# Linear attention and two feed-forward layers on one core: weighted sums made token by token, low parts on GpSimd, one written order for all engines

## The chip, the core and the metric

The kernel runs on one core of a Trainium2 chip. A core has five engines that run side by side, each through its own queue in order: PE (TensorE, matrix products and transposes), DVE (VectorE), ACT (ScalarE), POOL (GpSimd) and SP, which here only starts transfers. Products land in PSUM (eight banks of 128 partitions x 512 f32 numbers), everything else lives in SBUF. The metric is the time of one execution in microseconds (us) on the device.

## The reference

Attention without a softmax over tokens: queries and keys are turned into positive features, the keys' features are summed against v once per head, and every token's output is a weighted sum divided by its own denominator. Two feed-forward layers follow.

```python
batch, n_heads, seq, head_dim = (4, 8, 576, 64);  d_feat = 128
def phi(x):
    proj = np.einsum('bhsd,df->bhsf', x, w_phi)
    proj = proj - np.max(np.abs(proj), axis=-1, keepdims=True)
    return np.concatenate([np.exp(proj), np.exp(-proj)], axis=-1)
q_p, k_p = (phi(q), phi(k))
kv = np.einsum('bhsf,bhsd->bhfd', k_p, v)
z = np.sum(k_p, axis=2)
num = np.einsum('bhsf,bhfd->bhsd', q_p, kv)
den = np.einsum('bhsf,bhf->bhs', q_p, z)[..., None] + 1e-06
x = (num / den)                     # then batch and tokens become 2304 rows of 512
gate = 1.0 / (1.0 + np.exp(-(x @ w_gate)));  x = gate * (x @ w_val) @ w_out      # d_ff 1536
h = x @ w_in2;  out = np.maximum(0.01 * h, h) @ w_out2                           # d_ff 2048
```

## The kernel before

**Attention.** The work goes by pairs of heads, `B * KD` = 16 of them (four batches, four pairs each). Of a batch's 576 tokens 512 are the main part and 64 the remainder; the remainders of two pairs are handled together. For a pair: `t_main` transposes k and q (8 transposes, `ps_t`), ScalarE copies them to `x`; `p_k` and `p_q` project (`ps_p`), VectorE takes the largest magnitude (`m`, L337) and subtracts it (`t`, `tq`, L339), ScalarE takes Exp with both signs (`ka` for keys); `q_f` transposes the queries' differences (`ps_q`) and ScalarE writes the features `qf` from there; `kv_main` sums keys' features against v and a column of ones (`kv`, 36 short products, copied to `kvz`). Then `num` streams all 576 tokens through the summed matrix (`ps_n`, features already the right way round, 288 tokens a product, copied to `u`), `den` streams them through the column of sums (`ps_d`, copied to `dd` on VectorE). The denominators go round through memory: `norm1` stores four rows of `dd` into `d` with nine to a partition, `norm2` adds, inverts, stores to `rd` and reads it back spread over 64 partitions (`rb`), and GpSimd multiplies (L443). `norm3` splits the result into a high part in the reduced-precision type that PE multiplies at one pass (`xh`, ScalarE) and a low part (`xl`, VectorE, L51 by `split`).

**Gated units.** Every f32 product of the layers is made of three: high x high, high x low, low x high (`mm3`, L54 to L56). While attention runs, the first two hidden blocks (256 columns, `c` = 0) of layer one are made for batches 0 to 2 as soon as their x is ready (`moe_units`: `up1` into the banks `pg` and `pv`, `down1` into the same two), 216 products of 512 columns in all.

**Weights** arrive as 64-bit floats and are decoded in halves of a tile (`decode`: six operations on VectorE and two on ScalarE a half, of which the last, L115, makes the low part).

**Order.** `ORDERS` lists pieces by slot; it fixes the order of PE alone (`manual_schedule` with PE). A `d` asks for two decode steps, an `M` for one group of three gated products. The other engines' order comes from a scheduler. PSUM: two double banks (`pp`), two single ones (`at`), and `pg`, `pv`. After the stage the rest of layer one (from batch 3 of `c` = 0 on, `up_plain`, banks `ps_u`) and layer two follow; the change leaves their code alone.

Of the kernel before, what the change touches and what calls it, by code (L numbers as in the profile page):

```python
# [19 lines left out]
def linear_attention_moe(ctx, tc, q, k, v, w_phi, w_gate, w_val, w_out, w_in2, w_out2, out):  # L20
# [19 lines left out]
    ps_m = ctx.enter_context(tc.tile_pool(name="ps_m", bufs=1, space=PS))  # L40
# [6 lines left out]
    nc.scalar.activation(out=warm, in_=ebias, func=ACTF.Exp)  # L47
# [49 lines left out]

    def decode(raw, m, hi, lo, expo):
# [16 lines left out]
        nc.vector.tensor_tensor(out=lo, in0=mf, in1=hi.bitcast(F32), op=ALU.subtract)  # L115
        yield
# [11 lines left out]

    def decoded(keys, reserve, hold):
# [3 lines left out]
        raws = deque(fetch(keys[n // 2], n % 2, 3) for n in range(3))  # L133
        for n, key in enumerate(keys):
# [73 lines left out]
    def up1(c, b, h):  # L208
        w = bw[b]
        for f in range(CH):  # L210
            fs = slice(128 * f, 128 * f + 128)
            ps = []
            for i in range(2):
                p = ps_m.tile([128, 512], F32, tag=("pg", "pv")[i], name=("pg", "pv")[i])[:, :w]
                ps.append(p)
                wt = wts[1, c, i]
                for kk in range(KD):
                    yield kk
                    mm3(p, wt["vhi"][:, kk, fs], wt["vlo"][:, kk, fs], xpart(xh, b, kk), xpart(xl, b, kk), kk == 0, kk == KD - 1)
                if i == 0:  # L220
                    th = pools["tp"].tile([128, 512], F32, tag="th", name="th")[:, :w]
                    nc.scalar.activation(out=th, in_=p, func=ACTF.Tanh, scale=0.5)
            nc.vector.scalar_tensor_tensor(out=th, in0=th, scalar=1.0, in1=ps[1], op0=ALU.add, op1=ALU.mult)
            hidden(h, (f, b), th)
            yield KD - 1

# [11 lines left out]
    def down1(c, b, h):  # L238
        for e in range(KD):
            po = ps_m.tile([128, 512], F32, tag=("pg", "pv")[e % 2], name="po")[:, :bw[b]]  # L240
            for f in range(CH):
                if f:
                    yield 0
                mm_down1(po, wts[1, c, 2], b, e, h, f)
            first_sum(b, e, po, pools["tp"].tile([128, 512], F32, tag="st", name="st", bufs=2))
            yield
# [13 lines left out]
    def pair_bank(name):  # L260
        return ps_a.tile([128, 2, 512], F32, tag="pp", name=name, bufs=2)
# [20 lines left out]
    def load_pair(b, c):  # L282
        hs = slice(2 * c, 2 * c + 2)
        for nm, src, eng in (("k", k, nc.sync), ("q", q, nc.scalar if b == c == 0 else nc.sync)):
            t = ld.tile([128, J, 2, D], F32, tag=nm, name=nm)
            eng.dma_start(out=t, in_=src[b, hs, 0:MAIN, :].rearrange("h (p j) d -> p j h d", j=J))
            nat[nm, b, c] = t
            if (nm, b, c) == ("k", 0, 0):
                for h in range(2):
                    nc.gpsimd.dma_start(out=wbd[64 * h:64 * h + 64, h * NF:(h + 1) * NF], in_=w_phi)  # L290
        if c % 2 == 0:
            for nm, src in (("k", k), ("q", q)):
                t = ld.tile([128, 2, D], F32, tag=nm + "r", name=nm + "r", bufs=1)
                for h in range(2):
                    nc.sync.dma_start(
                        out=t[64 * h:64 * h + 64],
                        in_=src[b, 2 * c:2 * c + 4, MAIN:S, :].rearrange("(i h) s d -> h s i d", h=2)[h],
                    )
                nat[nm + "r", b, c // 2] = t
        vf = nat["v", b, c] = vfs[c % 2]  # L300
        nc.sync.dma_start(
            out=vf[:, 0:J].rearrange("p j (h w) -> p j h w", h=2)[:, :, :, 0:64],
            in_=v[b, hs, 0:MAIN, :].rearrange("h (p j) d -> p j h d", j=J),
# [4 lines left out]
    class Pair:  # L308
        pass

    rem = {}

    def t_main(p):
        ps = pair_bank("ps_t")
        for i, nm in enumerate("kq"):
            src = nat.pop((nm, p.b, p.c))
            for j in range(J):
                nc.tensor.transpose(ps[:, i, 128 * j:128 * j + 128], src[:, j].rearrange("p h d -> p (h d)"), ident)  # L318
        p.x = xt.tile([128, 2, MAIN], F32, tag="x", name="x", bufs=1)
        if TCOPY[p.i] == "D":  # L320
            nc.vector.tensor_copy(p.x, ps)
        else:
            nc.scalar.copy(p.x, ps)

    def t_rem(p):
        if p.c % 2:
            return
        ps = one_bank(256, "ps_tr")
        for i, nm in enumerate("kq"):
            nc.tensor.transpose(ps[:, 128 * i:128 * i + 128], nat.pop((nm + "r", p.b, p.c // 2)).rearrange("p i d -> p (i d)"), ident)  # L330
        rem["x"] = xt.tile([128, 256], F32, tag="xr", name="xr", bufs=1)
        nc.scalar.copy(rem["x"], ps)

    def centred(ps, shape, tag, bufs):

        m = wk.tile([128] + shape[:-1], F32, tag="m" + tag, name="m", bufs=2)
        nc.vector.tensor_reduce(out=m, in_=ps, axis=AX.X, op=ALU.max, apply_absolute_value=True)  # L337
        t = wk.tile([128] + shape, F32, tag=tag, name=tag, bufs=bufs)
        nc.vector.tensor_tensor(out=t, in0=ps, in1=m.unsqueeze(len(shape)).to_broadcast([128] + shape), op=ALU.subtract)  # L339
        return t  # L340

    def proj(x, tag):

        ps = pair_bank("ps_p")
        for j in range(J):
            for h in range(2):
# [156 lines left out]
    with tc.manual_schedule(engines={mybir.EngineType.PE}):  # L503
# [19 lines left out]
        for _ in m_gen:  # L523
            pass
# [463 lines left out]
```

## Time and profile before

| | |
|---|---|
| median of 3 runs | 1017.79 us (1016.29 to 1018.81) |
| the profiled execution | 1017.43 us, of which 1015.7 us are the span from first to last instruction |
| busy in the span | PE 982.6 us (97%), DVE 723.4 (71%), ACT 474.9 (47%), POOL 156.0 (15%) |
| granted TensorE clock | 0.995 of full speed on average |

The profiled execution lies 0.36 us under the median. 1.73 us lie outside its span. PE is nearly always busy on paper, but "busy" counts an instruction from its start to a modelled end, so products that follow one another overlap, and a PE that is slowed or handed work late can still look busy. How much work fits into a stretch is better read from the distance between starts.

### The profile page before, as it was taken

How to read it: one execution, taken by the hardware profiler on the slowest of the kernel's cores; microseconds unless marked ns; L12 is line 12 of the kernel's file. 1: busy time of each engine (PE TensorE's matmuls, PEld its weight loads, DVE VectorE, ACT ScalarE, POOL GpSimd, SP SyncE). 2: the span in 40 equal slices, each digit the busy share in tenths (PEclk: the TensorE clock that was granted, in tenths of full speed). 3: DMA queues.
4: the chain of work that ended last, by engine and by line, in shares of the span. 5: the costliest groups of instructions: out<-in, count | busy, mean ns of one | idle time of the engine just before them, and what ended most of it. 6: DMA issues, size and time to landing. Idle time of an engine off the chain costs nothing.

```text
span 1015.7 us, 16203 instructions
## 1 busy us (share of the span) xinstructions
PE 982.6 (97%) x6310; PEld 801.0 (79%) x6310; DVE 723.4 (71%) x1228; ACT 474.9 (47%) x817; POOL 156.0 (15%) x208
## 2 busy tenths in 40 slices
PE   7889899999999999999999999999999999999998
PEld 6556676777788888888888778788888888888886
DVE  4988555454587292974867679998878797978555
ACT  4766455545355344543544434665334343433221
POOL 1011011011002234143231312100101010101000
PEclk8999999999999999999999999999999999999999
DMA  7666444331699579496794956546334251614244
GB/s 191 165 180 160 127 132 111 99 96 46 213 328 282 77 204 179 92 288 100 158 268 71 228 187 248 193 146 201 130 119 165 84 193 56 228 43 165 65 153 136
DMA packets 118173, 160.15 MB, mean 158 GB/s; under 512 B 67504, under 2 KB 70064, under 8 KB 118096
## 3 DMA queue, kind: packets, MB, share of 16 engines
q1 hardware_dynamic: 92800, 93.75, 29.6%
q0 software_dynamic: 24256, 65.09, 25.5%
q8 instruction: 50, 0.82, 0.3%
q10 hardware_dynamic: 1040, 0.26, 0.1%
q14 instruction: 27, 0.22, 0.1%
HBM read 109.64 MB, written 49.36 MB: 157 GB/s over the span
## 4 chain that ended last, share of the span: by engine, by line
PE 75%; DVE 8%; issue 6%; DMA 5%; POOL 3%; ACT 2%; SPq 1%; POOLq 0%; DVEq 0%; ACTq 0%
PE ps_u L55 11%; PE ps_u L56 11%; PE ps_u L54 11%; PE ps_p L54 9%; PE ps_p L55 9%; PE ps_p L56 9%; PE ps_p L348 2%; DMA rb<-rd 2%; PE kv L387 2%; PE ps_n L415 2%; POOL accd L611 2%; DVE m L337 1%; PE ps_t L318 1%; POOL rb L443 1%; DMA w<-td 1%
## 5 line engine op out<-in xcount | busy, mean ns | idle before, releaser
L764 DVE TENSOR_TENSOR q<-ps_u,q 128x512 f32<-128x512 f32 x160 | 109.6, 686 | 63.6 <-PE ps_u L56 57.1
L54 PE MATMUL ps_u<-xh,w 128*128 128x512 f32 (+1 forms) x432 | 150.7, 350 | 1.2 <-ACT xh L50 1.1
L55 PE MATMUL ps_u<-xl,w 128*128 128x512 f32 (+1 forms) x432 | 151.4, 351 | 0.3 <-DVE xl L619 0.3
L56 PE MATMUL ps_u<-xh,w 128*128 128x512 f32 (+1 forms) x432 | 150.9, 350 | 0.0
L834 DVE TENSOR_TENSOR acc<-acc,ps_p 128x512 f32<-128x512 f32 x126 | 86.1, 683 | 39.6 <-PE ps_p L56 39.0
L54 PE MATMUL ps_p<-w,gh 128*128 128x512 f32 x288 | 112.2, 390 | 0.0
L55 PE MATMUL ps_p<-w,gh 128*128 128x512 f32 x288 | 112.0, 389 | 0.0
L56 PE MATMUL ps_p<-w,gl 128*128 128x512 f32 x288 | 111.6, 389 | 0.0
L611 POOL DMA_DIRECT2D accd<-w x80 | 70.7, 889 | 215.8 <-ACT w L610 139.8
L54 PE MATMUL ps_u<-w 128*128 128x512 f32 x256 | 100.4, 392 | 2.4 <-DVE q L764 2.4
L55 PE MATMUL ps_u<-w 128*128 128x512 f32 x256 | 100.0, 390 | 0.7 <-DMA w<-td 0.7
L56 PE MATMUL ps_u<-w 128*128 128x512 f32 x256 | 99.6, 389 | 0.0
L724 POOL DMA_DIRECT2D w<-td x88 | 48.0, 554 | 326.7 <-PE ps_u L56 303.0
L54 PEld LDWEIGHTS ps_u<-xh,w 128*128 128x128 f32 x432 | 81.5, 189 | 13.0 <-ACT xh L50 1.6
L55 PEld LDWEIGHTS ps_u<-xl,w 128*128 128x128 f32 x432 | 81.7, 189 | 12.1 <-DVE xl L619 0.7
L56 PEld LDWEIGHTS ps_u<-xh,w 128*128 128x128 f32 x432 | 81.7, 189 | 10.7
L650 ACT ACTIVATE q<-q 128x512 f32<-128x512 f32 x48 | 30.2, 632 | 113.1 <-DVE q L764 112.8
L54 PE MATMUL ps_p<-gh,w 128*128 128x512 f32 (+1 forms) x216 | 78.4, 366 | 1.9 <-DVE acc L614 1.9
L55 PE MATMUL ps_p<-gl,w 128*128 128x512 f32 (+1 forms) x216 | 78.9, 366 | 0.0
L56 PE MATMUL ps_p<-gh,w 128*128 128x512 f32 (+1 forms) x216 | 78.8, 366 | 0.0
L51 DVE TENSOR_TENSOR gl<-q,gh 128x512 fp32r<-128x512 f32 (+1 forms) x102 | 62.1, 619 | 21.2 <-ACT gh L50 20.7
L610 ACT COPY w<-ps_p 128x512 f32<-128x512 f32 (+1 forms) x80 | 43.3, 544 | 54.6 <-PE ps_p L56 47.7
(124 smaller groups left out, 1902.5 us busy)
## 6 DMA issues: line engine op xcount, KB each, us to landing
w<-td POOLq DMA_DIRECT2D x88, 512.0 KB, 6.3
td<-w SPq DMA_DIRECT2D x32, 512.0 KB, 3.1
accd<-w POOLq DMA_DIRECT2D x64, 256.0 KB, 6.1
raw<-in_moe_w_out_dram SPq DMA_DIRECT2D x28, 512.0 KB, 4.4
raw<-in_moe_w_in_dram SPq DMA_DIRECT2D x16, 512.0 KB, 4.0
raw<-in_moe_w_gate_dram SPq DMA_DIRECT2D x12, 512.0 KB, 5.7
raw<-in_moe_w_val_dram SPq DMA_DIRECT2D x12, 512.0 KB, 4.8
rb<-rd SPq DMA_DIRECT2D x32, 144.0 KB, 3.1
```

The lines of the kernel that those rows point to most:

```text
L51: nc.vector.tensor_tensor(out=lo, in0=src, in1=hi.bitcast(F32), op=ALU.subtract)
L54: nc.tensor.matmul(ps, lh, rh, start=first, stop=False, **kw)
L55: nc.tensor.matmul(ps, lh, rl, start=False, stop=False, **kw)
L56: nc.tensor.matmul(ps, ll, rh, start=False, stop=last, **kw)
L348: nc.tensor.matmul(ps[:, h, 128 * j:128 * j + 128], x[rows, 128 * j:128 * j + 128], wbd[rows, h * NF:(h + 1) * NF], start=True, stop=True)
L387: nc.tensor.matmul(ps[cs, s, h], p.kf[:, s, J * h + j, cs], vf[:, j, 64 * h:64 * h + 65], start=(s, h, j) == (0, 0, 0), stop=False, skip_g ...
L610: nc.scalar.copy(st, po)
L611: nc.gpsimd.dma_start(out=accd[b][:, e], in_=st, accum_op=ALU.add)
L650: nc.scalar.activation(out=th, in_=t, func=ACTF.Lrelu)
L724: nc.gpsimd.dma_start(out=ts[n][k][0].bitcast(F32), in_=td[l, pair, n][:, k])
L764: nc.vector.tensor_tensor(out=o, in0=x, in1=y, op=ALU.add)
L834: nc.vector.tensor_tensor(out=a, in0=a, in1=po, op=ALU.add)
```

## The change

- `num` and `den` become one step `om`: for blocks of 64 tokens the features are the operand that stays in the array, and the summed matrix with its column of sums (65 columns) streams through. A token's 64 sums and its denominator come out side by side on that token's partition: 32 + 4 products of 65 columns (in the trace, where an f32 product counts twice, 72) in place of 8 + 8 of 288.
- `rc` adds 1e-6 and inverts, `nm` scales the 512 main tokens on VectorE (`tn`), `nr` the remainder on ScalarE (`tr`), `ot` turns both back by PE (`ps_o`), and `xs_` copies them to `rb` (eight times VectorE, eight times ScalarE). The way through memory goes.
- The low parts `xl` (16 of 512 columns, 16 of 64) move from VectorE to GpSimd, and so do the low parts of the weights that are decoded during attention (10 halves). Six of the 16 copies of `x` move from ScalarE to VectorE.
- The gated units use the double banks too: three double banks and two single ones are all.
- `ORDER` is one list for all engines, with reduction, subtraction, Exp, copies, transfers and every decode operation (`d0` to `d7`) as pieces of their own. The decode is spread over the stage.
- The first k and q come by two queues, a head each, w_phi behind k.

```diff
-        nc.vector.tensor_tensor(out=lo, in0=mf, in1=hi.bitcast(F32), op=ALU.subtract)
+            lambda: (nc.gpsimd if timed[0] else nc.vector).tensor_tensor(out=lo, in0=mf, in1=hi.bitcast(F32), op=ALU.subtract),
...
-        return ps_a.tile([128, 2, 512], F32, tag="pp", name=name, bufs=2)
+        return ps_a.tile([128, 2, 512], F32, tag="pp", name=name, bufs=3)
...
+            for h, eng in enumerate((nc.sync, nc.scalar)):
+                eng.dma_start(out=t[:, :, h], in_=src[b, h, 0:MAIN, :].rearrange("(p j) d -> p j d", j=J))
+                if nm == "k":
+                    eng.dma_start(out=wbd[64 * h:64 * h + 64, h * NF:(h + 1) * NF], in_=w_phi)
...
-    def num(p):
-        ps = pair_bank("ps_n")
-        for s in range(2):
-            for n in range(2):
-                for h in range(2):
-                    nc.tensor.matmul(ps[COLS[h], n, 0:288], p.kvz[:, s, h, h:h + 64], p.qf[s][:, h, HALF[n]], start=s == 0, stop=s == 1)
-        p.u = wk.tile([128, 2, 288], F32, tag="u", name="u", bufs=2)
-        nc.scalar.copy(p.u, ps[:, :, 0:288])
-
...
+    def om(p):
+        p.psn = pair_bank("ps_n")
+        units = p.psn.rearrange("p b (u w) -> p (b u) w", u=2)
+        for j in range(J):
+            for h in range(2):
+                for s in range(2):
+                    for i in range(2):
+                        t0 = 128 * j + 64 * i
+                        nc.tensor.matmul(units[COLS[i], j, 65 * h:65 * h + 65], p.qf[s][:, h, t0:t0 + 64], p.kvz[:, s, h], start=s == 0, stop=s == 1)
         for s in range(2):
             for h in range(2):
-                z = p.kvz[:, s, h, 64 * (1 - h):64 * (1 - h) + 1].to_broadcast([128, 32])
-                for n in range(2):
-                    i = 2 * h + n
-                    nc.tensor.matmul(ps[32 * i:32 * i + 32], z, p.qf[s][:, h, HALF[n]], start=s == 0, stop=s == 1)
-        p.dd = wk.tile([128, 288], F32, tag="dd", name="dd", bufs=2)
-        nc.vector.tensor_copy(p.dd, ps)
-
-    def norm1(p):
-        p.d = wk.tile([128, 9], F32, tag="d", name="d", bufs=2)
-        nc.sync.dma_start(out=p.d, in_=p.dd[0:128:32, :])
-
-    def norm2(p):
-        r = wk.tile([128, 9], F32, tag="r", name="r", bufs=2)
-        nc.vector.tensor_scalar_add(p.d, p.d, 1e-6)
-        nc.vector.reciprocal(r, p.d)
-        rd = dr.tile([2, S], F32, tag="rd", name="rd", bufs=4)
-        nc.sync.dma_start(out=rd.rearrange("h (p e) -> (h p) e", e=9), in_=r)
+                nc.tensor.matmul(p.psn[COLS[h], 0, 130:195], p.qf[s][:, h, MAIN:S], p.kvz[:, s, h], start=s == 0, stop=s == 1)
+
+    def rc(p):
+        p.r = wk.tile([128, 10], F32, tag="r", name="r", bufs=2)
+        units = p.psn.rearrange("p b (u w) -> p (b u) w", u=2)
+        nc.vector.tensor_scalar_add(p.r[:, 0:8].rearrange("p (j h) -> p j h", h=2), units[:, :, 64:66], 1e-6)
+        nc.vector.tensor_scalar_add(p.r[:, 8:10], p.psn[:, 0, 130:195:64], 1e-6)
+        nc.vector.reciprocal(p.r, p.r)
+
+    def nm(p):
+        p.tn = wk.tile([128, J, 2, D], F32, tag="tn", name="tn")
+        units = p.psn.rearrange("p b (u w) -> p (b u) w", u=2)
+        nc.vector.tensor_tensor(
+            out=p.tn, in0=units[:, :, 0:132].rearrange("p j (h w) -> p j h w", h=2)[:, :, :, 0:64],
+            in1=p.r[:, 0:8].rearrange("p (j h) -> p j h", h=2).unsqueeze(3).to_broadcast([128, J, 2, D]), op=ALU.mult,
+        )
+
+    def nr(p):
+        p.tr = trs[p.i % 2]
+        nc.scalar.activation(out=p.tr[COLS[0], 0:64], in_=p.psn[COLS[0], 0, 130:194], func=ACTF.Copy, scale=p.r[COLS[0], 9:10])
+        nc.scalar.activation(out=p.tr[COLS[1], 64:128], in_=p.psn[COLS[1], 0, 131:195], func=ACTF.Copy, scale=p.r[COLS[1], 8:9])
+
+    def ot(p):
+        p.ps = pair_bank("ps_o")
+        for j in range(J):
+            nc.tensor.transpose(p.ps[:, 0, 128 * j:128 * j + 128], p.tn[:, j].rearrange("p h d -> p (h d)"), ident)
+        nc.tensor.matmul(p.ps[:, 1, 0:REM], p.tr, ident2, start=True, stop=True)
+
+    def xs_(p):
+        evict(UC[p.i], p.rb, p.ps.rearrange("p b t -> p (b t)")[:, 0:S])
...
+    def xhi(p):
+        nc.sync.dma_start(out=xd[p.b][:, p.c], in_=p.rb[:, 0:MAIN])
+        for src, hi, _ in x_parts(p):
+            nc.scalar.copy(hi, src)
+
+    def xlo(p):
+        for src, hi, lo in x_parts(p):
+            nc.gpsimd.tensor_tensor(out=lo, in0=src, in1=hi.bitcast(F32), op=ALU.subtract)
...
-    with tc.manual_schedule(engines={mybir.EngineType.PE}):
...
+    XC = "DAAADAAADDADDDAA"
+    UC = "DADADDDADADDAAAA"
+    ORDER = """
...
+        xc6 d5 M qr5 lr8 pk6 qb5 d6 om5 rk6 d7 sk6 f ea6 pq6 rc5 nm5 eb6 kv6 rq6 nr5 kw6 sq6 d0 ot5 kc6 lv8 d2 d1 qf6 xs5 d3 tr8
...
+        nm14 kw15 nr14 ot14 kc15 M xs14 M xh14 M xl14 M M M M t M s M h M l M M M M M t om15 s h l M rc15 nm15 M nr15 M ot15 c M
+        c xs15 M xh15 M xl15 M c c
...
+    with tc.manual_schedule():
+        for piece in ORDER.split():
+            nm = piece.rstrip("0123456789")
+            if nm == "d":
+                fine.append(int(piece[1:]))
+                ahead(1)
+            elif nm == "f":
+                fetch_next(order)
+            elif nm in gated:
+                gated[nm].popleft()()
+            else:
+                fns[nm](pair[int(piece[len(nm):])])
```

**PE at the weighted sums of the second pair** (names as above; `ps_tr` and `ps_pr` are the remainders' transposes and projections). Before:

```order
L348 MATMUL ps_p<-wbd,x 128x128 x8
L426 MATMUL ps_d<-qf,kvz 32x288 x8
L353 MATMUL ps_pr<-wbd,xr 128x256
L415 MATMUL ps_n<-qf,kvz 64x288 x8
L318 MATMUL ps_t<-ident,k 128x128 x4
```

And now:

```order
L543 MATMUL ps_n<-kvz,qf 64x65 x32
L546 MATMUL ps_n<-kvz,qf 64x65 x4
L394 MATMUL ps_p<-wbd,x 128x128 x8
L498 MATMUL ps_q<-ident,tq 128x128 x8
L500 MATMUL ps_r<-ident,tqr 128x128
L571 MATMUL ps_o<-ident,tn 128x128 x4
L572 MATMUL ps_o<-ident_122,tr_127 128x64
L524 MATMUL kv<-vf_129,ka 64x65 x16
```

Sixteen long products have become 36 short ones, and five products (`ps_o`) that turn the result back follow them, with a projection and a turn of another pair between.

**VectorE in the early part of the stage**, around the denominators (`e`, `m`, `w`, `raw` belong to the decode). Before:

```order
L337 TENSOR_REDUCE m<-ps_p 128x8
L112 SCALAR_TENSOR_TENSOR m<-m,e 128x512
L339 TENSOR_TENSOR tq<-ps_p,m 128x1024
L51 TENSOR_TENSOR xl_82<-rb,xh_81 128x512
L51 TENSOR_TENSOR xl_98<-rb,xh_97 128x64
L436 TENSOR_SCALAR d<-d 128x9
L115 TENSOR_TENSOR w<-m,w 128x512
L437 RECIPROCAL r<-d 128x9
```

And now:

```order
L381 TENSOR_REDUCE m<-ps_p 128x8
L551 TENSOR_SCALAR r<-ps_n 128x8
L552 TENSOR_SCALAR r<-ps_n 128x2
L553 RECIPROCAL r<-r 128x10
L386 TENSOR_TENSOR tq<-ps_p,m 128x1024
L558 TENSOR_TENSOR tn<-ps_n,r 128x512
L104 TENSOR_SCALAR e<-raw 128x512
```

The low parts (`xl`, `w`) have left this queue; the scaling `tn` has come in, and it stands behind a subtraction of another pair.

GpSimd's 16 rows of L443 in this stage are gone; in their place stand 10 rows of L111 on `w` and 32 of L590 on `xl`, in the order in which the pairs and the decode come to them.

## Rows read from the trace of the kernel before

**Rows 1.** Busy time by stretch (from:to, length, engines, clock, transfers).

```profile
7.20:25.40 18.20, 15.26 (x184) 12.57 (x185) 12.14 (x18) 9.73 (x15) 0.00 (x0) 0.81 0.86 213
25.40:101.60 76.20, 64.64 (x825) 46.18 (x822) 69.29 (x121) 51.42 (x89) 7.09 (x5) 0.98 0.62 168
101.60:254.00 152.40, 146.71 (x1693) 107.86 (x1693) 75.05 (x121) 81.44 (x140) 14.52 (x10) 1.00 0.38 102
264.60:1015.70 751.10, 741.84 (x3548) 622.99 (x3548) 566.08 (x966) 328.27 (x568) 130.33 (x176) 1.00 0.58 167
```

The engines stand in the order PE, PE's weight loads, DVE, ACT, POOL; then the granted clock, the transfer engines' share and GB/s.

**Rows 2.** The chain that ended last, 155 to 200 us: start, duration, what.

```profile
155.22 0.23 PE pg L55
155.69 1.11 PE ps_p L348 x16
...
162.06 3.02 DMA rd<-r
...
165.64 3.28 DMA rb<-rd
169.07 1.77 POOL rb L443
...
171.96 2.16 PE ps_n L415 x16
...
177.00 1.11 PE ps_d L426 x16
...
181.27 0.87 PE ps_t L318 x8
182.15 1.08 PE kv L387 x32
183.23 0.22 PE kv L389 x4
183.45 0.93 PE kv L387 x32
...
184.61 1.04 PE ps_q L397 x8
```

**Rows 3.** Timeline, first transposes and end of the stage: start, duration, instruction, [idle before].

```profile
6.62 0.30 PE L330 MATMUL ps_tr<-ident,kr 128*128 128x128 f32 x1 [0.89 <-DMA kr<-in_k_dram]
...
256.92 0.40 PE L54 MATMUL ps_u<-xh,w 128*128 128x512 f32 x1
...
262.46 1.42 POOL L443 TENSOR_TENSOR rb<-u,rb 128x576 f32<-128x576 f32 x1 [10.26 <-DMA rb<-rd]
...
264.58 0.97 PE L54 MATMUL ps_u<-xh,w 128*128 128x512 f32 x3 [1.14 <-ACT xh L50]
```

**Rows 4.** Groups on VectorE, 0 to 264.6 us: busy us, mean ns, idle before.

```profile
L337 DVE TENSOR_REDUCE m<-ps_p 128x8 f32<-128x1024 f32 x32 | 39.0, 1217 | 33.5 <-PE ps_p L348 33.5
L51 DVE TENSOR_TENSOR xl<-rb,xh 128x512 fp32r<-128x512 f32 x16 | 11.0, 688 | 27.2 <-ACT xh L50 27.2
L108 DVE SCALAR_TENSOR_TENSOR m<-raw,m 128x512 f32<-128x512 uint32 x12 | 8.1, 685 | 0.0
L337 DVE TENSOR_REDUCE m<-ps_pr 128x2 f32<-128x256 f32 x16 | 6.7, 416 | 7.8 <-PE ps_pr L353 7.5
L103 DVE TENSOR_SCALAR e<-raw 128x512 int32<-128x512 int32 x14 | 5.9, 421 | 4.1 <-DMA raw<-in_moe_w_gate_dram 3.4 <-DMA raw<-in_moe_w_val_dram 0.7
```

**Rows 5.** Decode line L112: durations least, median, most; first and last start.

```profile
L112 DVE SCALAR_TENSOR_TENSOR m<-m,e x12: 677/683/1765, 25.8 to 98.6; 128x512 f32<-128x512 f32 x12
```

**Rows 6.** The page's groups: a 128x512 operation on VectorE that reads PSUM.

```profile
L764 DVE TENSOR_TENSOR q<-ps_u,q 128x512 f32<-128x512 f32 x160 | 109.6, 686 | 63.6 <-PE ps_u L56 57.1
```

**Rows 7.** GpSimd beside VectorE at 39 us, and GpSimd's later low parts.

```profile
39.09 1.76 DVE L112 SCALAR_TENSOR_TENSOR m<-m,e 128x512 f32<-128x512 f32 x1
...
38.90 1.42 POOL L443 TENSOR_TENSOR rb<-u,rb 128x576 f32<-128x576 f32 x1 [35.52 <-DMA rb<-rd]
...
L619 POOL TENSOR_TENSOR xl<-acc,xh x8: 1294/1512/2265, 605.9 to 638.0; 128x512 fp32r<-128x512 f32 x8
```

More of the change, by code (lines that the diff above doesn't have):

```diff
@@ L206, in linear_attention_moe @@
     accd = {}
[L208 to L225, printed above, removed]
     def first_sum(b, e, po, st):
@@ L236, in mm_down1 @@
         mm3(po, wt["vhi"][:, f, es], wt["vlo"][:, f, es], *h[f, b], f == 0, f == CH - 1)
-    def down1(c, b, h):
-        for e in range(KD):
[L240 to L246, printed above, removed]
+    gated = {kind: deque() for kind in "Mtshlc"}
@@ new lines, in load_rem, with load_v @@
+    def load_rem(p):
+        b, c = p.b, p.c
+        for nm, src in (("k", k), ("q", q)):
+            t = ld.tile([128, 2, D], F32, tag=nm + "r", name=nm + "r", bufs=1)
+            for h in range(2):
+                nc.sync.dma_start(
+                    out=t[64 * h:64 * h + 64],
+                    in_=src[b, 2 * c:2 * c + 4, MAIN:S, :].rearrange("(i h) s d -> h s i d", h=2)[h],
+                )
+            nat[nm + "r", p.i] = t
+    def load_v(p):
+        b, c = p.b, p.c
+        vf = p.vf = vfs[c % 2]
@@ new lines, in tt, with xa, xb, xc @@
+    def tt(p):
+        p.ps = pair_bank("ps_t")
+        turn(p, 0)
+        turn(p, 1)
+    def xa(p):
+        p.x = xt.tile([128, 2, MAIN], F32, tag="x", name="x", bufs=1)
+        nc.scalar.copy(p.x[:, 0], p.ps[:, 0])
+    def xb(p):
+        nc.scalar.copy(p.x[:, 1], p.psb[:, 1])
+    def xc(p):
+        p.x = xt.tile([128, 2, MAIN], F32, tag="x", name="x", bufs=1)
+        evict(XC[p.i], p.x, p.ps)
+    def tr(p):
+        rem["ps"] = one_bank(256, "ps_tr")
+        for i, nm in enumerate("kq"):
+            nc.tensor.transpose(rem["ps"][:, 128 * i:128 * i + 128], nat.pop((nm + "r", p.i)).rearrange("p i d -> p (i d)"), ident)
@@ new lines, in xr, with pk, rk, sk @@
+    def xr(p):
+        rem["x"] = xt.tile([128, 256], F32, tag="xr", name="xr", bufs=1)
+        nc.scalar.copy(rem["x"], rem["ps"])
+    def pk(p):
+        p.psk = proj(p.x[:, 0])
+    def rk(p):
+        p.mk = absmax(p.psk, "t")
+    def sk(p):
+        p.t = centre(p.psk, p.mk, "t")
+    def ea(p, s=0):
+        if p.kf is None:
+            p.kf = wk.tile([128, 2, 2 * J, NF], F32, tag="ka", name="ka")
+        nc.scalar.activation(out=p.kf[:, s], in_=p.t, func=ACTF.Exp, scale=scales[s])
@@ new lines, in eb, with pkr, rkr, skr @@
+    def eb(p):
+        ea(p, 1)
+    def pkr(p):
+        rem["psk"] = proj_rem(0)
+    def rkr(p):
+        rem["mk"] = absmax(rem["psk"], "tr")
+    def skr(p):
+        rem["t"] = centre(rem["psk"], rem["mk"], "tr")
+    def er(p, s=0):
+        if rem.get("of") is not p:
+            rem["of"] = p
+            rem["k"] = wk.tile([128, 2, 2, NF], F32, tag="kar", name="kar")
+        nc.scalar.activation(out=rem["k"][:, s], in_=rem["t"], func=ACTF.Exp, scale=scales[s])
+    def es(p):
+        er(p, 1)
@@ new lines, in qf, with q_feat, qr, qa @@
+        p.psr = one_bank(128, "ps_r")
+        nc.tensor.transpose(p.psr, rem["q"][:, p.c % 2], ident)
+    def q_feat(p):
+        if p.qf is None:
+            p.qf = [wk.tile([128, 2, S], F32, tag="qf", name="qf", bufs=4) for _ in range(2)]
+        return p.qf
+    def qr(p):
+        for t, sc in zip(q_feat(p), scales):
+            nc.scalar.activation(out=t[:, :, MAIN:S], in_=p.psr.rearrange("p (h t) -> p h t", h=2), func=ACTF.Exp, scale=sc)
+    def qa(p, s=0):
+        nc.scalar.activation(out=q_feat(p)[s][:, :, 0:MAIN], in_=p.ps, func=ACTF.Exp, scale=scales[s])
@@ L532, in linear_attention_moe @@
     ps_b = ctx.enter_context(tc.tile_pool(name="ps_b", bufs=1, space=PS))
[L533 removed]
+    banks = {"u": [(ps_b, f"u{i}") for i in range(5)], "p": [(ps_b, f"p{i}") for i in range(3)]}
     turn = {"u": 0, "p": 0}
```

355 lines of the change are left out of this document (189 added, 166 removed), and 19 rows, old and new, of the table ORDERS.

## The prediction

> **What bounds the kernel now.** The busy times by stretch come first [rows 1]. The change works only up to the first product of the rest of layer one (`ps_u`), which starts at 256.92 us [rows 3]; the 751.1 us after 264.6 keep their code, and PE is busy for 741.8 of them. So the question is how fast attention, with 216 gated products in it, gets through PE.
>
> Until 101.6 us it is VectorE that sets the pace: it works 69.29 of 76.20 us in the second stretch, PE shows 64.64. From there to 254 us PE is busy for 146.71 of 152.40 us and VectorE for 75.05. Why VectorE is full early is seen in one decode line: all its 12 runs of the stage start between 25.8 and 98.6 us [rows 5]. Six pairs' features and 12 halves of a weight tile meet there.
>
> How much PE work is it? The chain of waits gives the time from start to start [rows 2]: eight transposes 0.87, a projection 1.11 (two a pair), `kv` from 182.15 to 184.61, so 2.46, the queries' turn 1.04 for eight and by that 0.13 for the ninth, denominators 1.11, weighted sums 2.16, a gated product 0.23. A pair without remainders is 0.87 + 2.22 + 2.46 + 1.17 + 1.11 + 2.16 = 9.99 us. Two transposes and four records of 256 columns for every second pair I put at 0.22 + 4 x 0.23 = 1.1 (a record streams as long as 512 columns of a gated product, an estimate from that row), 0.55 a pair. 16 x 10.54 + 216 x 0.23 = 168.6 + 49.7 = 218.3 us. The first transposes run at 6.62 and the last gated product ends at 256.9 [rows 3]: 250.3 us for 218.3 of work. **32 us of PE are lost**, besides the 6.6 at the start and 1.1 of waiting before 264.58, where PE wants the last pair's x, which came through `rb<-rd` and GpSimd's multiplication.
>
> **The change part by part.**
>
> *Products.* Out per pair: 1.11 + 2.16 = 3.27 us. In: `om`, 72 records of 65 columns. `kv` is of that very form (64 columns stay, 65 stream, two halves of the array in turn): 32 records take 0.93 to 1.08, 0.029 to 0.034 each, so 72 take 2.1 to 2.45; I take 2.4. `ot`: four transposes at 1.04 / 8 and one f32 product of two records, at most the same each: 0.52 + 0.26 = 0.8. So 3.2 for 3.27: PE's work stays at 217 us. Bounds: 2.1 + 0.52 gives 10 us less in 16 pairs; the other end, where the short products do not pair up, is a rival below.
>
> *The way through memory.* Out per pair: `rd<-r` 3.02, `rb<-rd` 3.28, GpSimd 1.77 in this chain [rows 2], plus the store before. Pairs further on cover it except at the end: there the wait of 1.14 us goes (the multiplication at 262.46, PE at 264.58 [rows 3]). In its place after the last `om`: three small operations, the scaling at 0.69 [rows 6], `ot`, a copy, a cast, a low part. Seven groups of gated products (4.8 us) stand behind that `om`, then 27 products of `ps_u` that need only older x, as now (6.2 us). That covers it; were the cover gone, some 5 us would show once.
>
> *VectorE.* Out per pair: the low part, 0.69 for 512 columns [rows 4], and per half tile another of the same form. In: scaling 0.69, three operations on ten columns or fewer (under 0.42 each by the 256-column row [rows 4]; I take 0.5 together), eight copies of 576 and six of 1024 columns at 1.22 or less [rows 4], 17 us or less. The stage's sum was 12.1 + 69.3 + 75.1 us [rows 1]; it loses 16 x 0.69 + 10 x 0.69 + two halves less of decode (2 x 3.6) = 25 and gains 11 + 8 + 17 = 36, so about 167 against PE's 217. What counts is where it lies. Early, a pair now needs four big operations (4.9), the remainders (0.8), scaling and denominators (1.2), copies (1.1) and one half tile of five operations, two of 0.42 and three of 0.68 (2.9): 10.9. Before, it was 4.9 + 0.8 + two half tiles of 3.6 + the low part and the denominators (1.5: 0.69 and two of at most 0.42): 14.4. PE needs 10.5 a pair there. So the early pairs go from about 14 to 11 us.
>
> *ScalarE* had 51.4 of 76.2 and 81.4 of 152.4 us [rows 1]. 15,360 columns of copies go (16 x 576, 6 x 1024), 6,656 come (8 x 576, 32 x 64): no more work, and PE covers it.
>
> *GpSimd* gets 26 low parts of 512 columns. Its later rows of that form take 1.29 to 2.27 us [rows 7], with the 16 small ones some 45 us of 230: covered. But it gets in VectorE's way: beside a multiplication on GpSimd, L112 took 1.76 us for its usual 0.68 [rows 5, 7]. If every one of the 26 cost VectorE that 1.08, it would be 28 us; VectorE would come to 195, still under 217. If one in three meets an operation that reads SBUF twice, it is 9 us, off the path. The Trainium skill speaks against this step: its page GPSIMD Engine Reference, section Key points, says that GpSimd shares its SBUF interfaces with VectorE, with contention when VectorE reads two SBUF inputs, and that VectorE is structurally about twice as fast at elementwise work. The trace agrees on both (1.76 for 0.68; 1.29 or more for 0.69). If that rule decides here, rival 2 comes true and its 1011 us; if the reserve of the two engines does, the 992 below.
>
> *Three double banks.* Eight uses share them. A pair holds them about 19 us in sum (each time the products, then what empties the bank: two passes of 1.22 behind a projection, and so on). A gated unit takes one bank most of the time from the seventh pair on, which leaves 19 / 2 = 9.5 us a pair, against 10.5 + 5 of PE work. Fits by half as much again; a rival below.
>
> *Start.* k comes as two halves by two queues, ahead of the remainders; first transposes at about 5 us for 6.6. Estimate from the remainders' order in the queue; bounds 4 and 7.
>
> **Sum.** First `ps_u` = start 5 + work 217 + losses. Losses: from 101.6 to 254 us, with VectorE half idle, PE was idle for 5.7 of 152.4 us, 3.7% [rows 1]; on 217 that is 8. While the first pairs fill up, I keep half of what the stretch 7.2 to 25.4 loses: 2.9 idle, and a clock of 0.81 (part of it at 1.2 GHz), another 3.5 [rows 1], so about 3. That gives 233 for 256.9, 24 us less, and 1.1 for the wait at the end: 25. The later part stays: it starts with two halves of decode less, 7 us of VectorE, of which 566 of 751 us are in use. From the profiled execution, 1017.4 (its median is 1017.8): **992 us**. With losses from 3 (only the fill) to 20 (8% and 3), and `om` at its lower bound: 980 to 1003.
>
> **The rivals.**
>
> 1. *Banks or the fixed order bind.* Now every engine follows one list; a late eviction holds PE, which cannot take the next piece. For: eight users on three banks, and VectorE waits 33.5 us for projections already [rows 4]. Against: 50% reserve. If it costs 1 us a pair, 1008 us. Chance 0.12.
> 2. *GpSimd holds VectorE up where VectorE is full.* In the first six pairs some three operations a pair move to GpSimd; if each costs VectorE 1.08 us [rows 7], a pair takes it 14.1 instead of 10.9, six pairs 19 us more: 1011. For: VectorE's early 10.9 is already over PE's 10.5, so nothing covers it there. Against: of 16 multiplications in the stage before, L112's median of 0.68 [rows 5] says that few met one. Chance 0.08.
> 3. *Slower: the 72 short products do not pair up.* If each ran as a transpose's record does, 0.13 us [rows 2], `om` would take 9.4 for 2.4 us: 112 us more, 1104. It decides from 0.055 us a record on, where `om` is 1.6 us a pair above the sum and the gain is gone. Against: `kv` has the form and runs at 0.03. What differs is that two, not four, products lie between two that add to the same place. Chance 0.06.
> 4. *PE without any gap after the start.* 5 + 210 us, 40 less: 977. For: the list orders everything; against: the old list left 3.7% even where VectorE was free. Chance 0.08.
>
> **Numbers.** The forecast (980 to 1003) has 0.66. 0.3% of 1017.8, 3 us, is about what a measurement of this kernel can tell from no change. Faster by more than that: 0.66, rival 4's 0.08 and rivals 1 and 2 but for 0.04 where they cost twice their price, 0.90. Slower: rival 3 and a quarter of that 0.04, 0.07. Same 0.03. To hold 8 in 10 the range takes in the lesser half of rivals 1 and 2: 980 to 1009.
>
> **What would show it.** First `ps_u` at 225 to 243 us; `om` at 2.1 to 2.5 us from start to start; VectorE under 85% busy before 100 us and the decode spread over the stage; PE idle under 5% from the seventh pair on; the stretch after the stage as long as before within 2 us. Wrong would be: `om` over 3.9 us, `ps_u` waiting for `xl`, or PE waiting for copies out of the double banks pair after pair.

## The result, and the profile after

Median 989.5 us (987.64 to 990.74, 4 runs) against 1018.3 us for the kernel before in the same comparison (1016.29 to 1020.53, 4 runs): ratio 0.9715, 95% interval 0.9689 to 0.9742. Faster by 2.8%, and 2.5 us under the forecast of 992. The profiled execution took 988.91 us, 986.8 of them the span.

The page of the changed kernel: busy us with share and instructions, then tenths of busy time in 40 slices of 24.7 us.

```profile
PE 965.0 (98%) x7040; PEld 819.8 (83%) x7040; DVE 727.7 (74%) x1218; ACT 474.4 (48%) x836; POOL 173.6 (18%) x236
...
PE   8899999999999999999999999999999999999998
...
DVE  5898678626982838839747699987979797978555
...
PEclk9999999999999999999999999999999999999999
```

PE and the clock are full from the third slice on. Busy time by stretch, columns as in [rows 1]:

```profile
4.85:25.40 20.55, 17.91 (x329) 15.61 (x328) 14.81 (x21) 12.55 (x22) 0.00 (x0) 1.00 0.84 199
...
25.40:101.60 76.20, 72.99 (x1318) 64.92 (x1319) 67.13 (x101) 54.83 (x100) 18.70 (x18) 1.00 0.63 150
...
101.60:160.00 58.40, 56.06 (x912) 50.35 (x909) 40.23 (x60) 36.38 (x71) 9.17 (x11) 1.00 0.47 121
160.00:225.50 65.50, 64.70 (x907) 56.01 (x904) 33.25 (x58) 36.52 (x69) 10.95 (x12) 1.00 0.16 52
...
227.27:986.80 759.53, 749.52 (x3576) 629.55 (x3576) 571.95 (x978) 331.51 (x571) 131.70 (x176) 1.00 0.59 169
```

Against [rows 1], PE is busy for 72.99 of the 76.20 us where it was for 64.64, and VectorE is hardly less full: 67.13 us for 69.29. The clock, 0.81 in the first stretch before, is granted whole.

The timeline of PE at the start, at the first weighted sums and at the end of the stage:

```profile
4.85 0.60 PE L406 MATMUL ps_t<-ident,k 128*128 128x128 f32 x4
...
20.18 2.08 PE L543 MATMUL ps_n<-kvz,qf 128*64 128x65 f32 x64
22.09 0.40 PE L546 MATMUL ps_n<-kvz,qf 128*64 128x65 f32 x8
22.33 1.10 PE L524 MATMUL kv<-vf,ka 128*64 128x65 f32 x32
...
222.35 0.60 PE L571 MATMUL ps_o<-ident,tn 128*128 128x128 f32 x4
222.79 0.33 PE L572 MATMUL ps_o<-ident,tr 128*128 128x64 f32 x2
222.93 0.48 PE L52 MATMUL ps_d<-gh,w 128*128 128x512 f32 x1
...
225.54 0.40 PE L54 MATMUL ps_d<-gh,w 128*128 128x512 f32 x1
227.27 0.50 PE L52 MATMUL ps_u<-xh,w 128*128 128x512 f32 x1 [1.32 <-ACT st L228]
```

`om` takes 22.33 - 20.18 = 2.15 us from start to start, `ot` 222.93 - 222.35 = 0.58 (in other pairs up to 0.75). The first `ps_u` starts at 227.27 us for 256.92 [rows 3]: 29.65 us earlier. Behind it 759.53 us pass, where it was 1015.7 - 256.92 = 758.78. So the whole gain lies in the stage, and 0.75 us is given back after it.

Where in the stage? The reductions on VectorE show how far the pairs are (two to a pair). VectorE's groups from 25.4 to 101.6 us, changed kernel:

```profile
L381 DVE TENSOR_REDUCE m<-ps_p 128x8 f32<-128x1024 f32 x14 | 17.1, 1218 | 3.3 <-PE ps_p L394 3.3
...
L109 DVE SCALAR_TENSOR_TENSOR m<-m,e 128x512 f32<-128x512 f32 x5 | 4.5, 894 | 0.1
```

and the kernel before in the same stretch:

```profile
L337 DVE TENSOR_REDUCE m<-ps_p 128x8 f32<-128x1024 f32 x11 | 13.4, 1215 | 0.0
L112 DVE SCALAR_TENSOR_TENSOR m<-m,e 128x512 f32<-128x512 f32 x12 | 10.3, 860 | 0.0
```

Seven pairs in place of five and a half: 76.2 / 7 = 10.9 us a pair for 13.9. VectorE spends 67.13 / 7 = 9.6 us on a pair, before 69.29 / 5.5 = 12.6, the halves of decode included.

### The profile page after: what moved, and what is told of

It reads as the page before. It is cut to its first block, busy times and chain, and to the rows that moved or that the text cites. A ratio compares the mean times of both kernels' runs of the same rounds, so it can differ in the third digit from the quotient of the medians.

```text
span 986.8 us, 17558 instructions
## 1 busy us (share of the span) xinstructions
PE 965.0 (98%) x7040; PEld 819.8 (83%) x7040; DVE 727.7 (74%) x1218; ACT 474.4 (48%) x836; POOL 173.6 (18%) x236
```

## The experiments

The theory at the start was the prediction's: before 101.6 us PE starved because VectorE was full, and the change takes work off it there. Each ratio below is to the kernel before on the same chip. The last column is the start of the first `ps_u` in the profile, the end of the stage.

| kernel | ratio, 95% interval | us from the changed kernel's ratio | first `ps_u` |
|---|---|---|---|
| changed | 0.9715 (0.9689 to 0.9742) | 0 | 227.27 |
| before: no trip | 0.9998 (0.9978 to 1.0018) | | 254.33 |
| before: low parts on GpSimd | 1.0049 (1.0029 to 1.0068) | | 258.42 |
| before: decode cut | 1.0155 (1.0122 to 1.0189) | | 266.83 |
| before: third bank | 1.0038 (1.0017 to 1.0058) | | 258.94 |
| before: third bank and cut | 1.0060 (1.0037 to 1.0083) | | 261.38 |
| changed: decode early | 0.9859 (0.9828 to 0.9891) | +14.6 | 240.56 |
| changed: low parts on VectorE | 0.9760 (0.9731 to 0.9789) | +4.6 | 231.81 |
| changed: list for PE alone | 0.9950 (0.9933 to 0.9967) | +23.9 | 248.05 |
| changed: VectorE's order free | 0.9846 (0.9821 to 0.9872) | +13.3 | 239.35 |
| changed: ScalarE's order free | 0.9733 (0.9709 to 0.9756) | +1.8 | 227.51 |
| changed: old first loads | 0.9703 (0.9684 to 0.9723) | -1.2 | 226.98 |
| changed: two small edits | 0.9729 (0.9705 to 0.9752) | +1.4 | 227.78 |

The third column is the difference of the ratios times 1016 us. Up to about 4 us of it may be chance, as the intervals show. The last column is one execution of each kernel; for the early decode, the low parts on VectorE and VectorE's free order it is the longest of four, by 1.4, 3.9 and 3.3 us over the next.

### Parts of the change, one at a time, in the kernel before

**The trip through memory.**

```diff
-        nc.sync.dma_start(out=p.d, in_=p.dd[0:128:32, :])
+        nc.vector.tensor_scalar_add(p.d, p.dd[:, 0:9], 1e-6)
...
-        nc.gpsimd.tensor_tensor(out=p.rb, in0=p.u.rearrange("p n t -> p (n t)"), in1=p.rb, op=ALU.mult)
+        nc.gpsimd.tensor_tensor(out=p.rb.rearrange("p (n t) -> p n t", n=2), in0=p.u, in1=p.dd.unsqueeze(1).to_broadcast([128, 2, 288]), op=ALU.mult)
```

> The kernel before without the way of the denominators through memory: three transfers a pair go, VectorE adds and inverts nine columns of dd where it lies, and GpSimd multiplies u by dd in place of by the inverse that came back (so the output is not the quotient; PE's order and every engine's work stay). Theory (PE lost its 32 us to a VectorE that was full before 101.6 us): the trip was hidden but for the 1.1 us at the end, so 1 to 3 us less than before. Rival (the trip's 6.3 us and GpSimd's wait for it starved the pairs behind): most of the 24 us of the stage, 15 to 25 less.

No difference. The trip was hidden. Whether the 1.1 us of its wait at the end were gained is under what can be told.

**Low parts on GpSimd.**

```diff
-        nc.vector.tensor_tensor(out=lo, in0=mf, in1=hi.bitcast(F32), op=ALU.subtract)
+        (nc.gpsimd if stage[0] else nc.vector).tensor_tensor(out=lo, in0=mf, in1=hi.bitcast(F32), op=ALU.subtract)
...
-        split(p.rb[:, 0:MAIN], xpart(xh, b, c), xpart(xl, b, c))
+        split(p.rb[:, 0:MAIN], xpart(xh, b, c), xpart(xl, b, c), nc.gpsimd)
```

> The kernel before with one part of the change alone: the low parts of x and those of the weights decoded in the stage go from VectorE to GpSimd. Theory: some 16 of the 26 lie before 101.6 us, where VectorE sets the pace; at 0.69 us that is 11 us off a full engine, so 5 to 11 us less than before. Rival (GpSimd holds VectorE up, 1.08 us where two meet, the second rival of the prediction): no gain, 0 to 10 more.

0.5% slower, some 5 us: the theory missed, the sign too. The first `ps_u` starts 1.5 us later than before, although 26 operations of 512 columns have left VectorE. The time lies in the rival's range, but this is not VectorE being held up to the point of doing less: it is busy for less of the stretch than before, and PE runs at a lower clock.

```profile
25.40:101.60 76.20, 62.97 (x771) 46.21 (x768) 63.13 (x103) 49.03 (x84) 28.17 (x23) 0.91 0.63 170
```

VectorE has 63.13 us for 69.29 in [rows 1], with operations that GpSimd held up counted at their longer times; the clock is 0.91 for 0.98. At half speed for 2 x 0.09 x 76.2 = 14 us PE loses about 7, an estimate, before about 1.5. So much of the loss can have come by the clock; which wait of PE led to it is not shown.

**VectorE's decode cut.** Four of six operations of a half are left out for twelve halves.

```diff
+        if count[0] > 12:
             nc.vector.tensor_scalar(out=m, in0=high, scalar1=0xFFFFF, ...)
             ...
+        else:
+            mf = ef
```

> The kernel before with most of VectorE's decode left out for the first twelve halves: of six operations a half the first and the last stay, the four between (0.42 + 3 x 0.68 = 2.46 us) go, so those weights are wrong; nothing else changes. Theory: 12 x 2.46 = 29.5 us come off VectorE before 101.6 us, an early pair falls from 14.4 to 9.5 us of VectorE, below PE's 10.5, and the kernel gets 15 to 24 us faster, almost the whole gain of the change, with two double banks, with the trip through memory and with PE's old order. Rival (banks, order or the trip hold PE): within 4 us of before.

The strongest miss: 1.6% slower. The stretch in question, columns as above:

```profile
25.40:101.60 76.20, 65.57 (x806) 46.31 (x808) 46.49 (x78) 48.02 (x83) 5.62 (x4) 0.91 0.63 166
```

VectorE works 46.49 of 76.20 us, and PE gets less done: nine reductions start in the stretch, before eleven. The clock is 0.91 here too, again some 14 us at 1.2 GHz, before 3 (0.98 in [rows 1]). One wait of PE is seen in the timeline of ScalarE and PE:

```profile
52.05 0.75 ACT L106 ACTIVATE e<-e,ebias 128x512 int32<-128x512 int32 x1
52.83 0.62 ACT L121 CAST w<-e 128x512 fp32r<-128x512 f32 x1
53.85 2.00 ACT L368 ACTIVATE ka<-t 128x1024 f32<-128x1024 f32 x2 [0.41 <-DVE t L347]
55.76 0.36 ACT L399 COPY kvz<-kv 128x260 f32<-128x260 f32 x1
...
53.30 0.40 PE L397 MATMUL kv<-vf,kar 128*64 128x130 f32 x4
56.17 1.94 PE L434 MATMUL ps_d<-qf,kvz 128*32 128x288 f32 x16 [2.48 <-ACT kvz L399]
58.04 2.01 PE L356 MATMUL ps_p<-wbd,x 64*128 64x128 f32 x16
```

The last product of `kv` ends at 53.30 + 0.40 = 53.70 us. The copy `kvz` stands behind two Exp of another pair, for whose `t` ScalarE waits first, and starts at 55.76. PE's list has the denominators next, so PE stops for 2.48 us; they then take 58.04 - 56.17 = 1.87 us from start to start, where it is 1.11 in [rows 2], with the clock at 0.66 from 55 to 60 us. So taking work off a full VectorE does not by itself make this kernel faster. How much of the 1.6% is the clock, and how much the new order that the scheduler gives the other engines once the decode is thinner, is not shown. The second theory: PE starves when what it needs next stands, in another engine's queue, behind work that can wait.

**A third double bank.** In the first six slots, in the space of `pg` and `pv`.

```diff
+        uses[0] += 1
+        if ps_e and uses[0] % 3 == 0:
+            return ps_e[0].tile([128, 2, 512], F32, tag="pe", name=name)
         return ps_a.tile([128, 2, 512], F32, tag="pp", name=name, bufs=2)
```

> The kernel before with one part of the change alone: a third double bank for the first six slots, in the space of pg and pv, whose four groups of gated products of those slots are made at the end; everything else stays, VectorE's decode as dense as before. Theory of the banks (before 105 us PE waited, where its releaser is the last reader of a double bank, 2.4 for t, 2.2 for u, 1.2 for x and 0.8 us for qf, more after a fall of the clock): 5 to 12 us less than before. Theory of VectorE's load alone: within 3 us of before.

Both edits, this one and the cut of the decode, in one kernel:

> The third double bank and the cut of VectorE's decode together in the kernel before (the cut leaves out four of six operations for twelve halves, so those weights are wrong). If banks and VectorE's load are both needed, and each hides the other: 12 to 24 us less than before, although the cut alone gave 15 more. If the scheduler's order on ScalarE and VectorE is what holds PE: no gain, 0 to 15 more than before.

0.4% and 0.6% slower. The bank alone, 3.9 us more, lies outside both ranges, the nearer of which was 3 us; the two together, 6.1 more, lie in that of the scheduler's order. Neither bank nor load, alone or together, brings a gain over the kernel before while the queues of the other engines keep the scheduler's order. The bank is not without effect, though: with VectorE relieved it takes back 9.7 us of the 15.8 that the cut alone costs (1.0060 for 1.0155), more than chance.

### Parts of the change undone in the changed kernel

**Decode early, in the list.** `d` and `f` pieces move, nothing else:

```diff
-        lv2 sq1 ea1 tr2 d0 om0 xc2 d2 lk4 d3 xr2 eb1 lr4
-        d1 kv1 rc0 nm0 kw1 d4 nr0 d5 f ot0 kc1 lv3 d6 qf1 xs0 d7 pqr2 xh0 pk2 rv2 qa1 xl0 sv2 d0 pq2 d2 qr1 qb1
+        lv2 sq1 ea1 tr2 d0 om0 xc2 d2 lk4 xr2 d1 eb1 lr4 d3 kv1 rc0 d4 nm0 kw1 d5 f nr0 ot0 d6
+        kc1 lv3 d7 qf1 xs0 d0 pqr2 xh0 d2 pk2 rv2 d1 qa1 xl0 d3 sv2 pq2 d4 qr1 qb1 d5 f
```

> The changed kernel with the ten halves of decode of the stage spread over pairs 2 to 6 only, as densely as before, in the same list; everything else stays. Theory: four halves (five operations, 2.9 us each on VectorE) come to the 79 us in which VectorE already works 70, so 4 to 12 us more than the changed kernel, about 993 to 1001, and the first gated products as late. Rival (the place of the decode does not matter since PE is the bound all along): within 1 us of the changed kernel.

14.6 us, a little over the top of the range. Its row and its reductions from 25.4 to 101.6 us (two views):

```profile
25.40:101.60 76.20, 63.60 (x1065) 55.92 (x1065) 67.51 (x105) 51.45 (x96) 24.37 (x22) 0.93 0.57 142
```

```profile
L381 DVE TENSOR_REDUCE m<-ps_p 128x8 f32<-128x1024 f32 x11 | 13.4, 1221 | 4.6 <-PE ps_p L394 4.5
L109 DVE SCALAR_TENSOR_TENSOR m<-m,e 128x512 f32<-128x512 f32 x9 | 6.9, 766 | 0.2
```

Nine halves in place of five, and the pairs are back at five and a half, the pace of before, with part of it by the clock (0.93). VectorE spends 67.51 / 5.5 = 12.3 us on a pair again. So in a list, too, decode that is dense early costs time, as the first theory has it. Whether by its load or because it stands ahead of work that PE waits for (2.4 us of this stretch for `tn`, where the changed kernel has no such wait) this run does not separate.

**Low parts back on VectorE.**

```diff
-            nc.gpsimd.tensor_tensor(out=lo, in0=src, in1=hi.bitcast(F32), op=ALU.subtract)
+            nc.vector.tensor_tensor(out=lo, in0=src, in1=hi.bitcast(F32), op=ALU.subtract)
```

> The changed kernel with the low parts of x and of the ten decoded halves back on VectorE, in the same places of the same list. Theory of VectorE's load, as left by the run with the early decode (11.6 us more on VectorE early cost 13 us): six halves and some six pairs lie before 101.6 us, 6 x 0.69 + 6 x (0.69 + 0.21) = 9.5 us on a VectorE that works 70 of 79 us there, so 5 to 12 us more than the changed kernel, 994 to 1001. Rival (VectorE has room, or gains back what GpSimd took from it: low parts on GpSimd alone made the kernel before 0.5% slower): within 3 us of the changed kernel, or below it.

4.6 us more by the ratio. The intervals of the two kernels overlap (0.9731 to 0.9742), and the stage that is 231.81 - 227.27 = 4.5 us longer is read from the longest of four executions (994.42 us; the others 989.96 to 990.50). So a gain of this part in the list is possible, and not shown. Seven pairs' reductions still fit into the stretch from 25.4 to 101.6 us, with VectorE busy for 69.99 us of it and PE for 70.89 (72.99 in the changed kernel). Under the scheduler the same move had cost 0.5%.

**The list for PE alone.**

```diff
-    with tc.manual_schedule():
+    with tc.manual_schedule(engines={mybir.EngineType.PE}):
```

> The changed kernel with its list kept for PE alone; VectorE, ScalarE, GpSimd and the transfers go by the scheduler again, as before. Banks, products and low parts on GpSimd stay. If the written order of the other engines is what keeps PE fed (copies that PE waits for stand right behind what they copy, decode spread out): 10 to 30 us more than the changed kernel, with PE waiting for copies by ScalarE and VectorE. If the third double bank, PE's own order and the products made the gain: within 4 us of the changed kernel.

Products, banks, GpSimd's part and PE's order stay, and 23.9 of the 29 us are lost. PE's waits up to 245 us (sum, times, longest):

```profile
PE ps_n L543 <- ACT kvz L533: 4.5, 2, 4.1
PE ps_q L498 <- DVE tq L386: 4.3, 4, 1.2
PE ps_o L571 <- DVE tn L558: 3.1, 4, 1.2
PE ps_o L571 <- ACT tr L566: 3.0, 3, 1.4
```

Which engine's order? Two kernels free one each, with the same edit and the other engines in the set.

> The changed kernel with its list for all engines but VectorE, whose order goes by the scheduler again; ScalarE's steps of the decode and the weights' transfers stay in their places, so the decode stays spread. If the spread of the decode is what counts on VectorE: within 4 us of the changed kernel. If the order of reductions, subtractions and scalings among themselves counts: 5 to 15 us more.

> The changed kernel with its list for all engines but ScalarE, whose order goes by the scheduler again. The list for PE alone cost 20.7 us of the 26 by the medians of its call (1010.2; before 1016.1), the early decode inside the list 13. If ScalarE's order is the other half (the copy kvz that PE waits for stands behind the next pair's Exp, 4.1 us in one wait with the list for PE alone): 5 to 12 us more than the changed kernel. If VectorE's order carries all: within 3 us.

VectorE's order is worth 13.3 us, ScalarE's nothing that can be told (1.8). With VectorE's order free PE waits for VectorE's results up to 240 us (sum, times, longest):

```profile
PE ps_n L543 <- DVE t L386: 4.7, 4, 1.9
PE ps_o L571 <- DVE tn L558: 3.2, 3, 2.0
PE ps_q L498 <- DVE tq L386: 2.3, 2, 1.8
```

In the changed kernel these are 1.9, none and 0.2 us up to the first `ps_u`. The difference, 8.1 us, is most of the 12.1 by which the stage is longer. How VectorE's order costs, with the work unchanged and the decode about where it was, is seen in one place, at 49 us:

```profile
49.10 0.16 DVE L551 TENSOR_SCALAR r<-ps_n 128x8 f32<-128x8 f32 x1
49.18 0.15 DVE L552 TENSOR_SCALAR r<-ps_n 128x2 f32<-128x2 f32 x1
49.24 0.68 DVE L107 SCALAR_TENSOR_TENSOR m<-raw,m 128x512 f32<-128x512 uint32 x1
49.84 0.21 DVE L553 RECIPROCAL r<-r 128x10 f32<-128x10 f32 x1
49.97 0.36 DVE L106 TENSOR_SCALAR m<-raw 128x512 int32<-128x512 int32 x1
50.25 0.68 DVE L558 TENSOR_TENSOR tn<-ps_n,r 128x512 f32<-128x512 f32 x1
...
50.99 0.66 PE L571 MATMUL ps_o<-ident,tn 128*128 128x128 f32 x4 [0.94 <-DVE tn L558]
```

Two operations of the decode, about 1 us, stand between the sums and the scaling; PE waits 0.94 us for `tn`. ScalarE's free order does no harm here, although one wait in the decode cut came from it. What differs is PE's list, in which `om` stands most of a pair behind the `kvz` that it needs; that this is the reason is argued, not shown.

**The first loads as before.**

```diff
-            for h, eng in enumerate((nc.sync, nc.scalar)):
-                eng.dma_start(out=t[:, :, h], in_=src[b, h, 0:MAIN, :].rearrange("(p j) d -> p j d", j=J))
+            eng = nc.scalar if p.i == 0 and nm == "q" else nc.sync
+            eng.dma_start(out=t, in_=src[b, hs, 0:MAIN, :].rearrange("h (p j) d -> p j h d", j=J))
...
```

> The changed kernel with the first loads as before: k of the first pair by SP's queue alone, q by ScalarE's, w_phi by GpSimd's. By the prediction's term of the start (first transposes at 4.85 in place of 6.62 us): 1.5 to 2 us more than the changed kernel. If the longer wait lets the granted clock fall to half as it did before from 14.7 to 21 us, up to 5 more. Rival (the first pairs wait for something else anyway): under 1 us.

```profile
5.67 1.12 PE L404 MATMUL ps_t<-ident,k 128*128 128x128 f32 x4 [0.41 <-DMA k<-in_k_dram]
...
226.98 0.50 PE L52 MATMUL ps_u<-xh,w 128*128 128x512 f32 x1 [1.38 <-ACT st L228]
```

The first transposes start 0.82 us later, the stage ends no later: the split of the first loads is worth nothing. The rest of the way from 6.62 to 4.85 us [rows 3] is order: k's transposes now stand ahead of the remainders', for which PE waited.

**A version to beat both.**

```diff
-    turn = {"u": 0, "p": 0}
+    turn = {"u": 2, "p": 0}
...
-        lk0 lr0 lv0 ta0 xa0 tb0 lk1 pk0 xb0
+        lk0 lr0 lk1 lv0 ta0 xa0 tb0 pk0 xb0
```

> A version that should beat both: the changed kernel with two small edits at waits that its profile shows. The banks of the rest of layer one start their turn two banks further on, away from the double bank whose last copy the first product waits 1.32 us for; and the second pair's k and q are loaded ahead of the first pair's v (PE waits 0.80 and 0.85 us for them at 11 and 12 us). If both waits were on the path: 1.3 to 3 us less than the changed kernel. If the wait is for the whole group of banks, or v comes late in its place: within 1 us.

No gain: the first `ps_u` waits 1.38 us for `st` as before, so the turn of the banks is not what it waits for. PE's waits for the early loads fall from 2.9 to 1.6 us, and those for VectorE's `tq` rise from 0.2 to 1.4. No version here beats the changed kernel by what can be told.

## Why the prediction was right, and where it was not

- *The sum.* The forecast was 5 + 217 + 11 = 233 us to the first `ps_u`; measured are 227.27. The start is 4.85. As to the work: with `om` at 2.15 for 2.4 and `ot` at 0.58 for 0.8, the 218.3 us of before lose 16 x (3.27 - 2.73) = 8.6, so it is 209.7, not 217. The losses are then 227.27 - 4.85 - 209.7 = 12.7, not 11. The mis-sized term is the products, by some 7.5 us (0.030 us a record, 2.15 / 72, at `kv`'s best and close to the lower bound given), or by some 5 if `ot` is taken at the 0.75 of its slower pairs. Losses larger by 1.7 us (less by the second reckoning) take part of it back, and so does the part behind the first `ps_u`, where 1.1 us of gain were forecast and 0.75 us are lost. So the total came within 2.5 us partly by errors that cancel.
- *"The early pairs go from about 14 to 11 us"* held to the tenth, 13.9 to 10.9. *"Until 101.6 us it is VectorE that sets the pace"* is the step that failed as a cause: in the kernel before, 23 us less VectorE work in that stretch made it slower, and in the changed kernel, with the low parts back on VectorE, seven pairs still fit while it is busy for 69.99 of 76.2 us, more than the 69.29 of before. A nearly full engine is not yet the bound. What the runs show in its place is the order of its work: freeing VectorE's order alone costs 13.3 us with its work unchanged, freeing all engines but PE 23.9. The place of the decode counts in the list as well (decode early: 14.6 us). The prediction priced the load alone; that the order held PE in the kernel before, too, is argued from this. Its sign "under 85% busy before 100 us" could not have told: VectorE is busy for 80.94 of the first 100 us, before for 80.17, and from 25.4 to 101.6 us for 67.13 / 76.2 = 88%, since more pairs fit.
- *Two sums in it are off.* VectorE's work up to the first `ps_u` was put at 167 us and is 155.76: the sum left out what goes with the old denominators, above all the copy `dd` (16 x 0.448 = 7.2 us), and the 64-column low parts (3.2 us). Nothing hung on it. The upper bound of 1003 needs a start at 7 us besides losses of 20; with the start of the sum it is 1001.
- *The way through memory* was hidden, as said. At the end PE no longer waits for x, but 1.32 us for the copy `st` of the gated sums out of a double bank, which the step left out: nothing gained there.
- *GpSimd* held VectorE up less than the 9 us taken. The three groups that show it most, 0 to 241 us:

```profile
L108 DVE SCALAR_TENSOR_TENSOR e<-raw,e 128x512 int32<-128x512 int32 x13 | 9.7, 746 | 8.3 <-ACT e L105 8.1
L109 DVE SCALAR_TENSOR_TENSOR m<-m,e 128x512 f32<-128x512 f32 x12 | 9.3, 774 | 0.3
L104 DVE TENSOR_SCALAR e<-raw 128x512 int32<-128x512 int32 x13 | 6.1, 466 | 10.6 <-DMA raw<-in_moe_w_out_dram 10.3 <-DMA raw<-in_moe_w_gate_dram 0.3
```

  At some 685 ns undisturbed, and 420 for the third [rows 4], that is 13 x 0.06 + 12 x 0.09 + 13 x 0.05 = 2.5 us. The rule of the Trainium skill that spoke against the step (GPSIMD Engine Reference, Key points: contention when VectorE reads two SBUF inputs) holds in single rows (L109, which has two, takes up to 1.67 us) and did not decide the time.
- *Three double banks* fit. From 101.6 to 225.5 us PE is idle for 3.14 of 123.9 us, 2.5% (3.7% was taken), with no wait for a bank pair after pair. The longest, 1.85 us of `ps_n` for `t` at 127.67 us, comes once. Alone the third bank gave nothing.
- *The start* was right in its number and worth nothing as a term: 0.8 us of it can be put back without loss. The clock fell in no stretch of the stage, where 3 us of fill with half its loss by the clock were kept; idle time took their place (2.64 us from 4.85 to 25.4).
- *Rivals.* The fixed order, feared in the first, is where most of the gain is. The second did not come; short products pair up (third); PE is not gapless (fourth): its rows show 2.64 + 3.21 + 3.14 + 1.32 = 10.3 us idle.

What stays open: how much each of the products, the third bank and PE's own order gives inside the 5 us that remain with the list for PE alone. Freeing VectorE and ScalarE one at a time costs 13.3 and 1.8 us, freeing all but PE 23.9; the rest lies with GpSimd and the transfers or with the combination, since the decode then lies early again (11 halves reach L109 from 25.4 to 101.6 us, for 5). Why the kernel before got slower with less VectorE work is shown only in single waits: every edit there also gave a new order of the scheduler. The new list with two double banks, and the old pieces in a list for all engines, were not tried.

## What to carry to other kernels

A busy share near the top says that an engine is a candidate, not that it is the bound: ask of each wait of the starving engine what stood ahead of the awaited result in its producer's queue, and whether that work could have waited. Where background work (a decode, a prefetch) shares a queue with work on the path, write its place out; here that was worth some 13 to 24 us, and the relief of the engine alone, under the scheduler's order, nothing. A gap on PE can cost twice: in the decode cut the granted clock was 1.00 from 50 to 53.7 us, and 0.54, near its lower level of 1.2 GHz, from 56.17 to 59.6, behind the 2.48 us without work. Not every gap does: behind the 1.85 us before 127.67 us in the changed kernel it stayed at 1.00.

## What was not expected of the hardware

An operation of VectorE with one input in SBUF is held up by GpSimd too, not only one with two. From the kernel before with low parts on GpSimd, the timeline of GpSimd and VectorE:

```profile
55.84 1.87 POOL L445 TENSOR_TENSOR rb<-u,rb 128x576 f32<-128x576 f32 x1 [2.19 <-DMA rb<-rd]
...
56.35 1.64 DVE L108 TENSOR_SCALAR m<-raw 128x512 int32<-128x512 int32 x1
```

It took 1.64 us where the same form takes 0.42 [rows 4], and it ended at 57.99, 0.28 us after GpSimd's operation (55.84 + 1.87 = 57.71). L105 of the same form did so twice more in this trace (1.27 us at 63.27, 1.39 us at 85.78, each ending 0.28 us after a GpSimd operation beside it). The prediction had counted only operations that read SBUF twice. The Trainium skill's page SBUF — State Buffer, section SBUF: two separate sides, says that VectorE and GpSimd take a port pair that they share as an exclusive lock for a whole instruction, VectorE for an operation in a two-port mode as well as for one with two SBUF inputs. These rows agree with it if the operation runs in such a mode, which the trace does not tell.
